# Offloaded exponentials on VectorE and GpSimd: a cubic without a quadratic term, fraction passes that either engine may run, GpSimd work in halves, and 73 packs in place of 65

## The chip, the cores and the metric

The kernel runs on one core of one Trainium2 chip. The metric is the device time of one execution in microseconds (us). Times below are medians of several executions. A ratio is computed as the mean time of one kernel's fast runs over that of the other's fast runs of the same rounds, so it is not quite the ratio of the medians. The study calls a run slow when it is over 1.5% longer than the fastest of its kernel.

A core has five engines that matter here. In this kernel TensorE multiplies matrices into PSUM. ScalarE evaluates the exponential. VectorE does elementwise work. GpSimd does elementwise work too, on SBUF tiles alone. SyncE issues DMAs. In the profile they are called PE, ACT, DVE, POOL and SP.

## The reference

Two attention branches share one input x (2048 x 512, 32 heads of 16) and are mixed by a gate. Branch A, softmax attention, is almost all of the work.

```
g = sigmoid((x * gate_w).sum(-1))
a = softmax_attention(x, A_wqkv, A_wo)      # 32 heads x 2048 x 2048 exponentials
b = linear_attention(x, B_wqkv, B_w_phi, B_wo)
out = g * a + (1 - g) * b
```

## The kernel before

Scores are computed in units of one head, 128 keys and 512 queries. For most units ScalarE takes the exponential straight from PSUM (`ps_ring` to `ET`), three units and two units in turn. That is 2048 units in all, too much for ScalarE alone to be fast: at the 0.452 us per unit that the profile below shows, an estimated 926 us. So four units at a time form a "pack" (128 x 2048) whose exponential is computed elsewhere, from the bits of the number. VectorE scales the scores into a 32-bit fixed-point number whose upper 16 bits are the exponent and whose lower 16 bits are the fraction (`EW`). GpSimd turns the upper half into bf16 bits (`ED`), VectorE extracts the fraction (`Ef`), evaluates a cubic in it (`Em`), and adds it to `ED`:

```python
ws.append(s.op("dve", 0.605, ... tensor_scalar(EW[i], bank, EC, 127*65536, mult, add)))   # x4, from PSUM
h  = s.op("pool", 1.9, ... tensor_scalar(ED, upper(EW), 128.0, EM, mult, add), ws, ...)   # integer part
f  = s.op("dve", 1.13, ... tensor_scalar(Ef, lower(EW), 2**-16, -EPHI, mult, add), ...)   # fraction
t  = s.op("dve", 0.6,  ... tensor_scalar(Em, Ef, E3, E2, mult, add))
u  = s.op("dve", 1.13, ... tensor_tensor(Em, Ef, Em, mult))
q  = s.op("dve", 0.6,  ... tensor_scalar(Em, Em, E1, add))
g_ = s.op("dve", 1.13, ... tensor_tensor(Em, Ef, Em, mult))
vs = s.op("dve", 1.13, ... tensor_tensor(ED, ED, Em, add), [g_, h])
...                                         # then TensorE multiplies ED with V
DVE_COUNT = (1, 1, 1, 2, 2, 2, 2, 1, 3, ...)      # packs in each of the 32 steps (4 heads x 512 queries); sum 65
```

(Abbreviated.) All instructions are placed by a planner that is part of the kernel. It is given a duration for each operation (the 0.605, 1.9, ... above), simulates the engines, and fixes the order of instructions on each engine when the kernel is built. The lists LEAD, PACE and BOUNDS say when work is released to it. In its plan a VectorE operation marked `port=True` and a GpSimd pass never run at the same time, and it holds GpSimd passes back until VectorE is about to do work that reads PSUM.

Two PSUM banks (`ps_mp`) serve everything but the main chain: the scores of packs, the projections, and the output matmuls.

The softmax here doesn't subtract the row's maximum and nothing guards it: scores larger than these inputs give would overflow.

## Time and profile before

| | before |
|---|---|
| time | 871.35 us (three runs, 870.81 to 872.87) |
| ScalarE busy | 842.7 us, 97% |
| VectorE busy | 796.9 us, 91% |
| GpSimd busy | 131.5 us, 15% |

The first part of the profile's page, the busy time of each engine with its share of the span, and the chain of work that ended last, by engine, for the kernel before:

```profile
PE 748.0 (86%) x5242; PEld 215.5 (25%) x5330; DVE 796.9 (91%) x1118; ACT 842.7 (97%) x783; POOL 131.5 (15%) x76
...
ACT 93%; PE 4%; DVE 1%; SPq 1%; DMA 1%; issue 0%; another core or an unknown queue 0%
```

The busy time alone would leave it open whether VectorE binds too. The chain does not: followed back from the last instruction, 93% of the span is ScalarE's own work. But the view by windows shows that VectorE has almost no room in the middle of the kernel (columns: window, its length, then the busy time of each engine, the clock, DMA share, GB/s):

```profile
core 0: us, PE busy (x) PEld busy (x) DVE busy (x) ACT busy (x) POOL busy (x), PEclk, DMA share, GB/s
...
200.00:300.00 100.00, 87.73 (x631) 25.36 (x640) 98.56 (x130) 100.00 (x103) 13.28 (x7) 1.00 0.01 3
...
600.00:700.00 100.00, 84.87 (x633) 25.23 (x642) 98.94 (x151) 100.00 (x93) 13.29 (x7) 1.00 0.02 6
```

Both engines are full there. What can be taken from ScalarE depends on what a pack costs VectorE. The groups of the page (line, engine, operation, tiles, shapes, count, then busy us, mean ns, and idle time before) give that cost:

```profile
L735 ACT ACTIVATE ET<-ps_ring 128x1536 bf16<-128x1536 f32 x715 | 817.5, 1346 | 10.8 <-PE ps_ring L718 9.2
...
L819 POOL TENSOR_SCALAR ED<-EW 128x2048 int16<-128x2048 int16 x65 | 124.4, 1915 | 717.4 <-DVE Em L829 101.5
L812 DVE TENSOR_SCALAR EW<-ps_mp 128x512 int32<-128x512 f32 x260 | 170.8, 680 | 11.7 <-PE ps_mp L808 9.0
...
L822 DVE TENSOR_SCALAR Ef<-EW 128x2048 f16<-128x2048 uint16 x65 | 83.3, 1282 | 0.5
L830 DVE TENSOR_TENSOR ED<-ED,Em 128x2048 uint16<-128x2048 int16 x65 | 81.3, 1251 | 0.5 <-POOL ED L819 0.2
L829 DVE TENSOR_TENSOR Em<-Ef,Em 128x2048 f16<-128x2048 f16 x65 | 81.1, 1247 | 0.5
L827 DVE TENSOR_TENSOR Em<-Ef,Em 128x2048 f16<-128x2048 f16 x65 | 79.3, 1220 | 0.4
...
L825 DVE TENSOR_SCALAR Em<-Ef 128x2048 f16<-128x2048 f16 x65 | 49.2, 757 | 0.4
L828 DVE TENSOR_SCALAR Em<-Em 128x2048 f16<-128x2048 f16 x65 | 47.3, 728 | 0.4
```

The seven VectorE groups add up to 592 us, or 9.1 us per pack. A pack takes four units of 512 columns from ScalarE. In steady state three units and two units follow each other every 2.26 us, so a unit costs ScalarE 0.452 us and a pack spares it 1.81 us.

The mean of 1282 ns for `Ef` hides two kinds. Here are three instructions from the timeline of the kernel before (start us, duration us, engine, line, operation), first of GpSimd, then of VectorE:

```profile
414.90 1.90 POOL L819 TENSOR_SCALAR ED<-EW 128x2048 int16<-128x2048 int16 x1 [10.57 <-DVE ED L830]
```

```profile
415.93 1.94 DVE L822 TENSOR_SCALAR Ef<-EW 128x2048 f16<-128x2048 uint16 x1
...
425.75 1.18 DVE L822 TENSOR_SCALAR Ef<-EW 128x2048 f16<-128x2048 uint16 x1
```

The pass at 425.75 us ran alone. The one at 415.93 us met a GpSimd pass and took 0.76 us longer; it ended 1.07 us after GpSimd did. I call this blocking. To count it, I took, for each group of equal instructions, the time above the group's lower quartile wherever it exceeded 60 ns: 21.2 us on VectorE in the kernel before. The 21.2 us lie on 28 VectorE instructions, each of which met a GpSimd pass. The `EW` passes, which read PSUM, show none of it: 120 of the 260 ran at least partly under a GpSimd pass, and none took over 0.693 us (median 0.681 us).

### The profile page before, as it was taken

To read this page: it belongs to the slowest core of one execution; us is meant where nothing else is said; L and a number is where in the kernel's file an instruction comes from. 1 tells how busy PE (TensorE), PEld (TensorE's weight loads), DVE (VectorE), ACT (ScalarE), POOL (GpSimd) and SP (SyncE) were. 2 spreads that over 40 slices of the span, in tenths; PEclk is the share of its full clock that TensorE was granted. 3 is DMA by queue.
4 is the path that set the end of the run, shared out by engine and by line. 5 is a ranking of instruction groups with operands and counts; after the bars stand their busy time and mean duration, and the time that the engine had idled before them with its cause. 6 is when DMAs were issued, how large, how long until landed. Compare 5 with 4: busy or idle time off the path is not lost.

```text
span 871.1 us, 12869 instructions
## 1 busy us (share of the span) xinstructions
PE 748.0 (86%) x5242; PEld 215.5 (25%) x5330; DVE 796.9 (91%) x1118; ACT 842.7 (97%) x783; POOL 131.5 (15%) x76
## 2 busy tenths in 40 slices
PE   6999998898888888888888888888788897878885
PEld 2323322222222222222222222222222221212221
DVE  2765799999999999979999998999999999999986
ACT  3999999999999999999999999999999999999995
POOL 3000111100110010120102111112100111212020
PEclk8999999999999999999999999999999999999998
DMA  5231000000000000000000000000000000000000
GB/s 109 62 76 52 4 4 3 2 4 5 3 2 4 4 4 8 10 10 10 4 2 9 4 17 9 5 3 2 4 4 10 10 10 8 3 4 4 4 1 25
DMA packets 25115, 11.21 MB, mean 13 GB/s; under 512 B 18016, under 2 KB 25056, under 8 KB 25056
## 3 DMA queue, kind: packets, MB, share of 16 engines
q1 hardware_dynamic: 23472, 9.99, 4.3%
q8 instruction: 42, 0.69, 0.3%
q10 hardware_dynamic: 1584, 0.39, 0.2%
q14 instruction: 17, 0.14, 0.1%
HBM read 3.16 MB, written 2.10 MB: 6 GB/s over the span
## 4 chain that ended last, share of the span: by engine, by line
ACT 93%; PE 4%; DVE 1%; SPq 1%; DMA 1%; issue 0%; another core or an unknown queue 0%
ACT ET L735 90%; ACT phi L958 4%; PE ps_ring L718 2%; PE ps_mp L605 1%; SPq L545 1%; PE ps_ot L763 1%; DMA xT<-in_A_x_dram 0%; DVE kvbd L938 0%; DMA out_dram<-outt 0%; DVE outt L1070 0%; DVE fsum L962 0%; DVE EW L812 0%; PE ps_ot L836 0%; DVE T L847 0%; PE ps_mp L896 0%
## 5 line engine op out<-in xcount | busy, mean ns | idle before, releaser
L735 ACT ACTIVATE ET<-ps_ring 128x1536 bf16<-128x1536 f32 x715 | 817.5, 1346 | 10.8 <-PE ps_ring L718 9.2
L718 PE MATMUL ps_ring<-qT,kT 64*128 64x512 bf16 x1788 | 357.1, 387 | 95.9 <-ACT ET L735 88.9
L819 POOL TENSOR_SCALAR ED<-EW 128x2048 int16<-128x2048 int16 x65 | 124.4, 1915 | 717.4 <-DVE Em L829 101.5
L812 DVE TENSOR_SCALAR EW<-ps_mp 128x512 int32<-128x512 f32 x260 | 170.8, 680 | 11.7 <-PE ps_mp L808 9.0
L763 PE MATMUL ps_ot<-ET,Vaug 128*17 128x512 bf16 x1788 | 176.1, 386 | 1.0 <-ACT ET L735 0.5
L718 PEld LDWEIGHTS ps_ring<-qT,kT 64*128 64x128 bf16 x1788 | 73.7, 93 | 300.2 <-ACT ET L735 260.2
L808 PE MATMUL ps_mp<-qT,kT 128*128 128x512 bf16 x221 | 83.2, 388 | 4.4 <-DVE EW L812 1.0
L822 DVE TENSOR_SCALAR Ef<-EW 128x2048 f16<-128x2048 uint16 x65 | 83.3, 1282 | 0.5
L830 DVE TENSOR_TENSOR ED<-ED,Em 128x2048 uint16<-128x2048 int16 x65 | 81.3, 1251 | 0.5 <-POOL ED L819 0.2
L829 DVE TENSOR_TENSOR Em<-Ef,Em 128x2048 f16<-128x2048 f16 x65 | 81.1, 1247 | 0.5
L827 DVE TENSOR_TENSOR Em<-Ef,Em 128x2048 f16<-128x2048 f16 x65 | 79.3, 1220 | 0.4
L763 PEld LDWEIGHTS ps_ot<-ET,Vaug 128*17 128x17 bf16 x1788 | 43.0, 87 | 141.4 <-issue 129.5
L825 DVE TENSOR_SCALAR Em<-Ef 128x2048 f16<-128x2048 f16 x65 | 49.2, 757 | 0.4
L828 DVE TENSOR_SCALAR Em<-Em 128x2048 f16<-128x2048 f16 x65 | 47.3, 728 | 0.4
L808 PEld LDWEIGHTS ps_mp<-qT,kT 128*128 128x128 bf16 x260 | 24.0, 96 | 64.0 <-issue 31.6
L964 DVE TENSOR_TENSOR phi<-phi,frec 128x1024 bf16<-128x1024 bf16 x32 | 39.2, 1225 | 0.1
L962 DVE TENSOR_REDUCE fsum<-phi 128x64 f32<-128x1024 bf16 x32 | 38.5, 1203 | 0.3 <-ACT phi L958 0.3
L605 PE MATMUL ps_mp<-xT,WA 128*128 128x512 bf16 x110 | 35.5, 388 | 3.7 <-DMA xT<-in_A_x_dram 2.5
L958 ACT ACTIVATE phi<-ps_mp 128x512 bf16<-128x512 f32 x64 | 38.6, 723 | 0.0
L605 PE MATMUL ps_mp<-Wp,xT 128*128 128x512 bf16 x115 | 37.4, 384 | 1.2 <-DVE EW L812 0.5
L662 DVE CAST Vaug<-ps_mp 128x128 bf16<-128x128 f32 (+1 forms) x32 | 13.4, 423 | 17.3 <-PE ps_mp L605 17.1
L847 DVE STREAM_TRANSPOSE T<-ps_ot 128x512 f32<-128x512 f32 x32 | 22.7, 710 | 6.7 <-PE ps_ot L763 6.2
(70 smaller groups left out, 425.7 us busy)
## 6 DMA issues: line engine op xcount, KB each, us to landing
out_dram<-outt SPq DMA_DIRECT2D x16, 128.0 KB, 1.7
qT<-qst SPq DMA_DIRECT2D x120, 16.0 KB, 1.8
WA<-in_A_wqkv_dram SPq DMA_DIRECT2D x3, 384.0 KB, 4.6
WBV<-in_B_wqkv_dram SPq DMA_DIRECT2D x1, 512.0 KB, 4.1
WoA<-in_A_wo_dram SPq DMA_DIRECT2D x1, 512.0 KB, 3.6
WoB<-in_B_wo_dram SPq DMA_DIRECT2D x1, 512.0 KB, 4.3
WA<-in_A_wqkv_dram ACTq DMA_DIRECT2D x3, 128.0 KB, 3.3
xT<-in_A_x_dram SPq DMA_TRANSPOSE x16, 2.7
```

The source lines that it names most:

```text
L605: m = s.op("pe", self.c_mm(n), lambda e, c=c: e.matmul(self.bk(b)[:, 0:n], lhs(c), rhs(c), start=(c == 0), stop=(c == 3)), deps if c == 0 ...
L718: return lambda e: e.matmul(self.ps_ring[:, x % RING, :], self.kT[r, g // 2, kt * P:(kt + 1) * P], self.qT[r, n % 2, i, :], start=True, st ...
L735: self.o_exp.append(s.op("act", w * 0.434 + 0.045, lambda e, b0=b0, s0=s0, w=w: e.activation(self.ET[:, s0:s0 + w, :], self.ps_ring[:, b0: ...
L763: return lambda e: e.matmul(self.ps_ot[32 * i:32 * i + VSL, :], self.Vaug[:, kt, h, :], self.ET[:, (4 * p + k) % NSLOT, :], start=(kt == 0 ...
L808: m = s.op("pe", self.c_mm(512), lambda e, i=i, b=b: e.matmul(self.bk(b), self.kT[:, cp, kt * P:(kt + 1) * P], self.qT[:, n % 2, i, :], st ...
L812: ws.append(s.op("dve", 0.605, lambda e, i=i, b=b: e.tensor_scalar(self.EW[:, ew.idx, i * QCH:(i + 1) * QCH], self.bk(b), float(EC), float ...
L819: h = s.op("pool", 1.9, lambda e: e.tensor_scalar(out().bitcast(dt.int16), half(1, dt.int16), 128.0, float(EM), op0=ALU.mult, op1=ALU.add) ...
L822: f = s.op("dve", 1.13, lambda e: e.tensor_scalar(self.Ef[:], half(0, dt.uint16), float(2.0 ** -16), -EPHI, op0=ALU.mult, op1=ALU.add), ws ...
L827: u = s.op("dve", 1.13, lambda e: e.tensor_tensor(self.Em[:], self.Ef[:], self.Em[:], ALU.mult), [t], pr, port=True)
L829: g_ = s.op("dve", 1.13, lambda e: e.tensor_tensor(self.Em[:], self.Ef[:], self.Em[:], ALU.mult), [q], pr, port=True)
L830: vs = [s.op("dve", 1.13, lambda e: e.tensor_tensor(out(), out().bitcast(dt.int16), self.Em[:], ALU.add), [g_, h], pr, port=True)]
L958: ex.append(s.op("act", 0.478, lambda e, sg=sg: e.activation(self.phi[:, ph.idx, :, sg, :], self.bk(b).rearrange("p (h f) -> p h f", f=DH) ...
```

## The change

The intent is to make a pack cheap enough on VectorE that eight more packs can be taken from ScalarE. There are five parts.

1. The cubic is expanded about its inflection point, so that it has no quadratic term: u(E1 + E3 u²) with u = fraction + 0.965. One scale-add pass on VectorE goes away; the constant moves into EM.
2. The fraction pass may run on GpSimd or VectorE (`alt=0.6`), whichever the planner finds free; `Ef` gets a second buffer.
3. GpSimd passes are issued in halves of 1024 columns.
4. 73 packs instead of 65, with new plan constants and new rules (RULES) for holding and releasing GpSimd passes.
5. The first of the eight output matmuls of a tile (seven and one in the last four tiles) waits for the operands of the whole sum.

```diff
-LEAD = [16.9408, 8.9394, 19.7683, 21.1253, 20.1566]
-PACE = [7.9948, 0.4589]
-BOUNDS = [5.8136, 10.5124, 10.0461, 26.2873]
+LEAD = [16.392310765238605, 9.228976317877777, 20.2802, 21.11011600354882, 19.952522408464993]
+PACE = [7.244074408835803, 0.4535348430560933]
+BOUNDS = [5.884433981907029, 10.4896, 10.2757, 27.4904]
+RULES = [0.9369, 0.1308, 0.8252]
-EM = 53
-EPHI = 0.49984589
-E1, E2, E3 = 125.48413, 43.840203, 9.9574722
+EM = -68
+EU = 0.96498297
+E1, E3 = 61.15205816, 9.99312212
-DVE_COUNT = (1, 1, 1, 2, 2, 2, 2, 1, 3, 2, 1, 3, 1, 2, 3, 1, 2, 3, 2, 2, 2, 2, 3, 2, 1, 3, 2, 2, 4, 1, 3, 3)
+DVE_COUNT = (1, 1, 1, 2, 2, 3, 2, 2, 2, 1, 3, 3, 1, 3, 3, 2, 2, 3, 3, 2, 3, 2, 2, 2, 4, 2, 3, 2, 3, 2, 3, 3)
 ... (planner: an operation may have a second engine; rules for releasing GpSimd passes)
-        h = s.op("pool", 1.9, lambda e: e.tensor_scalar(
-            out().bitcast(dt.int16), half(1, dt.int16), 128.0, float(EM), op0=ALU.mult, op1=ALU.add), ws, pr, ...)
-        f = s.op("dve", 1.13, ... self.Ef[:], half(0, dt.uint16), float(2.0 ** -16), -EPHI, ...)
-        t = s.op("dve", 0.6, lambda e: e.tensor_scalar(
-            self.Em[:], self.Ef[:], E3, E2, op0=ALU.mult, op1=ALU.add), [f], pr, port=True)
-        u = s.op("dve", 1.13, ... tensor_tensor(self.Em[:], self.Ef[:], self.Em[:], ALU.mult), [t], ...)
-        q = s.op("dve", 0.6, ... tensor_scalar(self.Em[:], self.Em[:], E1, None, op0=ALU.add), [u], ...)
+        fs = [s.op("pool", 0.98, lambda e, c=c: e.tensor_scalar(
+            self.Ef[:, ef.idx, W * c:W * c + W], half(0, dt.uint16, c), float(2.0 ** -16), EU,
+            op0=ALU.mult, op1=ALU.add), ws[2 * c:2 * c + 2], pr, alloc=[ef], frees=[ew], gate=gate, alt=0.6,
+            port=True) for c in range(2)]
+        hs = [s.op("pool", 0.98, ... self.ED half c ... ws[2 * c:2 * c + 2], ...) for c in range(2)]
+        u = s.op("dve", 1.13, lambda e: e.tensor_tensor(self.Em[:], Ef(), Ef(), ALU.mult), fs + [self.ed_prev], ...)
+        q = s.op("dve", 0.6, lambda e: e.tensor_scalar(
+            self.Em[:], self.Em[:], E3, E1, op0=ALU.mult, op1=ALU.add), [u], pr, port=True)
 ... (outputs)
-                    ... alloc=[b, *also] if k == 0 else (), order=[m], cols=512,
+                    ... alloc=[b, *also] if k == 0 else (), order=[m] if k else [x[3] for x in bl],
```

More of the change, by code (lines that the diff above doesn't have):

```diff
@@ L28 @@
 PASSES = 1
-LEAD = [16.9408, 8.9394, 19.7683, 21.1253, 20.1566]
-PACE = [7.9948, 0.4589]
-BOUNDS = [5.8136, 10.5124, 10.0461, 26.2873]
+LEAD = [16.392310765238605, 9.228976317877777, 20.2802, 21.11011600354882, 19.952522408464993]
+PACE = [7.244074408835803, 0.4535348430560933]
+BOUNDS = [5.884433981907029, 10.4896, 10.2757, 27.4904]
+RULES = [0.9369, 0.1308, 0.8252]
 VSL = 17
 EC = 0.25 * 1.4426950408889634 * 65536
-EM = 53
-EPHI = 0.49984589
-E1, E2, E3 = 125.48413, 43.840203, 9.9574722
-DVE_COUNT = (1, 1, 1, 2, 2, 2, 2, 1, 3, 2, 1, 3, 1, 2, 3, 1, 2, 3, 2, 2, 2, 2, 3, 2, 1, 3, 2, 2, 4, 1, 3, 3)
+EM = -68
+EU = 0.96498297
+E1, E3 = 61.15205816, 9.99312212
+DVE_COUNT = (1, 1, 1, 2, 2, 3, 2, 2, 2, 1, 3, 3, 1, 3, 3, 2, 2, 3, 3, 2, 3, 2, 2, 2, 4, 2, 3, 2, 3, 2, 3, 3)
 def dve_tiles(n):
-    return ((6,), (5, 11), (4, 8, 12), (3, 6, 9, 12))[DVE_COUNT[min(n, NN - 1)] - 1]
+    return ((6,), (5, 11), (4, 8, 12), (3, 6, 9, 12), (2, 5, 8, 11, 13))[DVE_COUNT[min(n, NN - 1)] - 1]
 class Buf:
@@ L61, in __init__ @@
         self.left = readers
+        self.war = ()
         self.last = []
@@ L73 @@
                  "ready", "seq", "dma", "order", "inc", "tick", "clock", "war", "cols", "lat", "cfg", "exp", "grp", "port",
-                 "gate", "go")
+                 "gate", "go", "alt", "run")
     def __init__(self, eng, dur, fns, deps, prio, rel, alloc, frees, dma, order, cols=0, cfg="F", port=False,
-                 gate=False):
+                 gate=False, alt=0.0, run=0.0):
         self.cols = cols
+        self.alt = alt
+        self.run = run or dur
         self.port = port or eng == "pool"
@@ L109, in __init__ @@
     def __init__(self):
+        self.SHY, self.REST, self.FILL = RULES
         self.ops = []
@@ L117, in op @@
     def op(self, eng, dur, fns, deps=(), prio=0.0, rel=0.0, alloc=(), frees=(), dma=0, order=(),
-           cols=0, cfg="F", port=False, gate=False):
+           cols=0, cfg="F", port=False, gate=False, alt=0.0, run=0.0):
         if not isinstance(fns, (list, tuple)):
@@ L122, in op @@
             cols = 90
-        o = Op(eng, dur, list(fns), deps, prio, rel, alloc, frees, dma, order, cols, cfg, port, gate)
+        o = Op(eng, dur, list(fns), deps, prio, rel, alloc, frees, dma, order, cols, cfg, port, gate, alt, run)
         if eng == "dve" and any(getattr(b.pool, "scarce", False) for b in o.frees):
@@ L173, in run, with at, push, release @@
         self.exps = [q.exp for q in self.chain]
-        def release(o):
+        def at(o, eng):
             r = o.rel
             for d in list(o.deps) + list(o.order):
-                if d.eng == o.eng and not d.dma:
-                    r = max(r, d.end + (self.RAW[o.eng] if d in o.deps else 0.0))
+                if d.eng == eng and not d.dma:
+                    r = max(r, d.end + (self.RAW[eng] if d in o.deps else 0.0))
                 else:
                     r = max(r, self.seen(d))
-            o.ready = r
-            heapq.heappush(future[o.eng], (r, o.seq, o))
+            return r
+        def push(o, when=0.0):
+            heapq.heappush(future[o.eng], (max(when, at(o, o.eng)), o.seq, o))
+            if o.alt:
+                heapq.heappush(future["dve"], (max(when, at(o, "dve") + self.SHY), o.seq, o))
+        def release(o):
+            o.ready = at(o, o.eng)
+            push(o)
         for o in self.ops:
@@ L191, in run @@
             for e in self.ENGS:
+                while ready[e] and ready[e][0][2].start is not None:
+                    heapq.heappop(ready[e])
+                while future[e] and future[e][0][2].start is not None:
+                    heapq.heappop(future[e])
                 if ready[e]:
@@ L206, in run @@
             now, e = best
+            if parked and not ready["dve"] and now >= t["dve"] and now >= hold["pool"] and (
+                    not future["dve"] or future["dve"][0][0] - now > self.REST * parked[0].dur):
+                c = parked.pop(0)
+                c.go = True
+                if last is not None:
+                    c.war.append(last)
+                heapq.heappush(future["pool"], (now, c.seq, c))
+                continue
             if e == "pe":
@@ L224, in run @@
                 c = it[2]
+                if c.start is not None:
+                    continue
                 if look is not None and c is not look[0]:
@@ L233, in run @@
                 if e == "pool" and c.gate and not c.go:
-                    parked.append(c)
+                    if c not in parked:
+                        parked.append(c)
                     continue
-                if e == "dve" and c.port and hold["pool"] > now + 0.02 and len(held) < 8:
+                if e == "dve" and c.port and hold["pool"] > now + 0.02:
                     held.append(it)
@@ L242, in run @@
                 continue
-            if e == "dve" and o is None and held:
-                o = held[0][2]
-                held = held[1:]
+            if e == "dve" and o is None:
+                for it in held:
+                    heapq.heappush(future[e], (hold["pool"], it[1], it[2]))
+                continue
             if o is None:
@@ L263, in run @@
                 if pool.free[0][0] > now:
-                    heapq.heappush(future[e], (pool.free[0][0], o.seq, o))
+                    push(o, pool.free[0][0])
                     ok = False
@@ L268, in run @@
                 continue
+            if e != o.eng:
+                o.eng, o.dur = e, o.alt
+                if o in parked:
+                    parked.remove(o)
             for b in o.alloc:
-                _, b.idx, war = b.pool.free.pop(0)
-                o.war.extend(war)
+                if b.idx is None:
+                    _, b.idx, b.war = b.pool.free.pop(0)
+                o.war.extend(b.war)
             if o.port:
@@ L276, in run @@
             if e == "dve":
-                while o.gate and parked:
-                    c = parked.pop(0)
-                    c.go = True
-                    if last is not None:
-                        c.war.append(last)
-                    heapq.heappush(future["pool"], (now + self.TAIL["dve"], c.seq, c))
+                if parked and not o.port:
+                    free = o.run + sum(x[2].run for x in ready[e] if not x[2].port and x[2].start is None)
+                    free -= max(0.0, hold["pool"] - now)
+                    while parked and free > self.FILL * parked[0].dur:
+                        c = parked.pop(0)
+                        c.go = True
+                        if last is not None:
+                            c.war.append(last)
+                        heapq.heappush(future["pool"], (now + self.TAIL["dve"], c.seq, c))
+                        free -= c.dur
                 last = o
@@ L307, in run @@
                     for q in b.pool.parked:
-                        heapq.heappush(future[q.eng], (ft, q.seq, q))
+                        push(q, ft)
                     b.pool.parked = []
@@ L462, in memory @@
         at("EW", [P, 2, 4 * QCH], dt.int32)
-        at("Ef", [P, 4 * QCH], dt.float16)
+        at("Ef", [P, 2, 4 * QCH], dt.float16)
         at("Em", [P, 4 * QCH], dt.float16)
@@ L489, in pools @@
         self.ED_p = BufPool(2)
+        self.Ef_p = BufPool(2)
         self.outt_p = BufPool(3)
@@ L802, in dve_pack @@
         pr = rel + LEAD[1]
-        ew, ed = Buf(self.EW_p, 2), Buf(self.ED_p, 1)
+        ew, ed, ef = Buf(self.EW_p, 4), Buf(self.ED_p, 1), Buf(self.Ef_p, 2)
         ws = []
@@ L813, in dve_pack @@
                 self.EW[:, ew.idx, i * QCH:(i + 1) * QCH], self.bk(b), float(EC), float(127 * 65536),
-                op0=ALU.mult, op1=ALU.add), [m], pr, frees=[b], gate=i < 2))
+                op0=ALU.mult, op1=ALU.add), [m], pr, frees=[b], run=0.605 * (4 - i)))
             self.qk_dve[n] = self.eq_prev = m
-        half = lambda k, t: self.EW[:, ew.idx, :].bitcast(t).rearrange("p (n two) -> p n two", two=2)[:, :, k]
+        W = 2 * QCH
+        half = lambda k, t, c: self.EW[:, ew.idx, W * c:W * c + W].bitcast(t).rearrange(
+            "p (n two) -> p n two", two=2)[:, :, k]
@@ L817, in dve_pack @@
         out = lambda: self.ED[:, ed.idx, :]
-        h = s.op("pool", 1.9, lambda e: e.tensor_scalar(
-            out().bitcast(dt.int16), half(1, dt.int16), 128.0, float(EM), op0=ALU.mult, op1=ALU.add), ws, pr,
-            alloc=[ed], frees=[ew], gate=(n, j) != (NN - 1, nj - 1))
-        f = s.op("dve", 1.13, lambda e: e.tensor_scalar(
-            self.Ef[:], half(0, dt.uint16), float(2.0 ** -16), -EPHI, op0=ALU.mult, op1=ALU.add),
-            ws + [self.ed_prev], pr, frees=[ew], port=True)
@@ L825, in dve_pack @@
-        t = s.op("dve", 0.6, lambda e: e.tensor_scalar(
-            self.Em[:], self.Ef[:], E3, E2, op0=ALU.mult, op1=ALU.add), [f], pr, port=True)
-        u = s.op("dve", 1.13, lambda e: e.tensor_tensor(self.Em[:], self.Ef[:], self.Em[:], ALU.mult), [t], pr, port=True)
-        q = s.op("dve", 0.6, lambda e: e.tensor_scalar(self.Em[:], self.Em[:], E1, None, op0=ALU.add), [u], pr, port=True)
-        g_ = s.op("dve", 1.13, lambda e: e.tensor_tensor(self.Em[:], self.Ef[:], self.Em[:], ALU.mult), [q], pr, port=True)
@@ L830, in dve_pack @@
-        vs = [s.op("dve", 1.13, lambda e: e.tensor_tensor(out(), out().bitcast(dt.int16), self.Em[:], ALU.add), [g_, h], pr,
-                   port=True)]
+        Ef = lambda: self.Ef[:, ef.idx, :]
+        gate = (n, j) != (NN - 1, nj - 1)
+        fs = [s.op("pool", 0.98, lambda e, c=c: e.tensor_scalar(
+            self.Ef[:, ef.idx, W * c:W * c + W], half(0, dt.uint16, c), float(2.0 ** -16), EU,
+            op0=ALU.mult, op1=ALU.add), ws[2 * c:2 * c + 2], pr, alloc=[ef], frees=[ew], gate=gate, alt=0.6,
+            port=True) for c in range(2)]
@@ new lines, in dve_pack @@
+        hs = [s.op("pool", 0.98, lambda e, c=c: e.tensor_scalar(
+            self.ED[:, ed.idx, W * c:W * c + W].bitcast(dt.int16), half(1, dt.int16, c), 128.0, float(EM),
+            op0=ALU.mult, op1=ALU.add), ws[2 * c:2 * c + 2], pr, alloc=[ed], frees=[ew], gate=gate)
+            for c in range(2)]
+        u = s.op("dve", 1.13, lambda e: e.tensor_tensor(self.Em[:], Ef(), Ef(), ALU.mult), fs + [self.ed_prev], pr,
+                 frees=[ef], port=True)
+        q = s.op("dve", 0.6, lambda e: e.tensor_scalar(
+            self.Em[:], self.Em[:], E3, E1, op0=ALU.mult, op1=ALU.add), [u], pr, port=True)
@@ L832, in dve_pack @@
+        g_ = s.op("dve", 1.13, lambda e: e.tensor_tensor(self.Em[:], Ef(), self.Em[:], ALU.mult), [q], pr,
+                  frees=[ef], port=True)
+        vs = [s.op("dve", 1.13, lambda e: e.tensor_tensor(out(), out().bitcast(dt.int16), self.Em[:], ALU.add),
+                   [g_] + hs, pr, port=True)]
         self.ed_prev = vs[-1]
@@ L1038, in mms @@
                     self.bk(b), src(), W[:, pr, :], start=(k == 0), stop=(k == len(bl) - 1)),
-                    [dep, self.d_woa, self.d_wob], prio, rel, alloc=[b, *also] if k == 0 else (), order=[m], cols=512,
-                    frees=[ba] if ba else ())
+                    [dep, self.d_woa, self.d_wob], prio, rel, alloc=[b, *also] if k == 0 else (), order=[m] if k else [x[3] for x in bl],
+                    cols=512, frees=[ba] if ba else ())
             return m
```

## The prediction

> **What bounds the kernel now.** ScalarE, with VectorE nearly as full. The page's busy table gives ScalarE 842.7 us of 871.1 (97%), VectorE 796.9 (91%), TensorE 748.0, GpSimd 131.5 (15%). The chain that ended last is 93% ScalarE (90% the exponential ET from ps_ring). From 100 to 840 us the windows view shows ScalarE 97 to 100%, VectorE 91 to 99% busy. So exponentials can be moved off ScalarE only if each offloaded pack first becomes cheaper on VectorE. In the timeline, a group of three and a group of two exponentials repeat every 2.26 us: 0.452 us per 512 columns.
>
> **VectorE cost per pack (65 packs), by the groups view.** Old: EW 4 passes, 170.8/65 = 2.63 us; Ef 1.28; Em scale-add 0.76; product 1.22; add 0.73; product 1.25; final add 1.25. Sum 9.1 us, 593 us in all. The new cubic, expanded at its inflection point, has no quadratic term: one scale-add pass goes, and the fraction pass Ef may run on GpSimd. New per pack: 2.63 + 1.22 + 0.73 + 1.25 + 1.25 = 7.1 us, plus about 1.4 us (estimate: two halves) if VectorE extracts the fraction. For 73 packs: 517 us with all fractions on GpSimd, 619 us with none. VectorE total between 721 and 823 us against 797 now. Likely about 760.
>
> **GpSimd.** Half of the 1.90 us pass is an estimated 0.98 us. Integer parts 73 x 1.96 = 143 us; with half of the fractions about 215 us. GpSimd stays below 35% busy, but blocks VectorE. [...] an Ef pass starting at 415.93 us, under a GpSimd pass (414.90 to 416.80), took 1.94 us instead of 1.18; a T product at 847.66 took 2.10 instead of 0.42. Means above the undisturbed durations give some 20 us of such blocking now; I expect 15 to 40 us after. VectorE can absorb that.
>
> **On the critical path.** Eight more packs take 32 x 512 columns from ScalarE: 32 x 0.452 = 14.5 us. All of it is on the chain, since ScalarE is the bottleneck throughout. The idle parts of ScalarE should stay: some 15 us before the first exponential, about 6 us of waits, about 11 us of tail after the last exponential. The VectorE relief only pays for the packs. TensorE work hardly changes. The changed ordering of the output matmuls keeps a half-done accumulation from blocking TensorE, worth at most 1 us.
>
> **Predicted: 856.5 us** (871.35 - 14.5, rounded), range 851 to 864. Chances: faster by over 2% (below about 854 us) 0.25; within 2% 0.72; slower 0.03.
>
> **What would show the steps right.** about 703 exponential instructions instead of 715; ScalarE busy near 828 us, share still 97%; the period still 2.26 us; ScalarE waits in the chain unchanged at 5 to 8 us; GpSimd busy 180 to 260 us; VectorE busy 745 to 800 us; one Em pass gone; Ef split between the engines.
>
> **What would make it wrong.** Slower: [...] packs or PSUM banks come late, TensorE stops in order at them, and ScalarE waits more than 10 us on ps_ring. Or GpSimd halves cost far over 0.98 us. Faster: the new plan also removes start-up waits or the stall near 323 us, where kvbd took 2.0 us and ScalarE then waited 1.6 us.

(The sum came to 871.35 - 14.5 = 856.9, put down as 856.5 us. Two durations were estimates. For half of the 1.90 us GpSimd pass it took 0.98 us; the changed kernel's trace shows 1.04 us. For a fraction extracted by VectorE in two halves it took 1.4 us, with `Ef` whole at a mean of 1.28 us; there the trace shows 2 x 0.68 us.)

## The result, and the profile after

The changed kernel took 855.85 us (four runs, 854.87 to 856.81) against 871.08 us for the kernel before. The ratio is 0.9825, with a 95% interval of 0.9811 to 0.9840. That is faster by 1.75%, clear of noise, and inside the predicted range.

| | before | after |
|---|---|---|
| time | 871.08 us | 855.85 us |
| span of the profiled run | 871.1 us | 854.7 us |
| ScalarE busy | 842.7 us | 828.2 us |
| ScalarE not busy (span less busy) | 28.4 us | 26.5 us |
| VectorE busy | 796.9 us | 767.0 us |
| GpSimd busy | 131.5 us | 280.1 us |
| time lost to blocking, VectorE / GpSimd | 21.2 / 1.1 us | 21.5 / 24.7 us |

The busy time of each engine and the chain that ended last, in the changed kernel:

```profile
PE 744.6 (87%) x5226; PEld 215.1 (25%) x5316; DVE 767.0 (90%) x1105; ACT 828.2 (97%) x771; POOL 280.1 (33%) x250
...
ACT 92%; PE 4%; DVE 1%; SPq 1%; POOL 1%; DMA 1%; issue 0%; ACTq 0%
```

The groups that answer to those shown of before:

```profile
L774 ACT ACTIVATE ET<-ps_ring 128x1536 bf16<-128x1536 f32 (+1 forms) x703 | 803.0, 1345 | 8.6 <-PE ps_ring L757 8.0
...
L865 POOL TENSOR_SCALAR ED<-EW 128x1024 int16<-128x1024 int16 x146 | 173.8, 1199 | 322.6 <-DVE Em L873 64.1
L851 DVE TENSOR_SCALAR EW<-ps_mp 128x512 int32<-128x512 f32 x292 | 192.4, 680 | 25.3 <-PE ps_mp L847 18.3
L861 POOL TENSOR_SCALAR Ef<-EW 128x1024 f16<-128x1024 uint16 x93 | 99.3, 1067 | 235.0 <-DVE EW L851 58.0
...
L869 DVE TENSOR_TENSOR Em<-Ef 128x2048 f16<-128x2048 f16 x73 | 93.6, 1282 | 2.8 <-POOL Ef L861 2.5
L875 DVE TENSOR_TENSOR ED<-ED,Em 128x2048 uint16<-128x2048 int16 x73 | 92.4, 1266 | 2.5 <-POOL ED L865 2.3
L873 DVE TENSOR_TENSOR Em<-Ef,Em 128x2048 f16<-128x2048 f16 x73 | 92.8, 1271 | 0.6
...
L871 DVE TENSOR_SCALAR Em<-Em 128x2048 f16<-128x2048 f16 x73 | 55.7, 763 | 0.2
...
L861 DVE TENSOR_SCALAR Ef<-EW 128x1024 f16<-128x1024 uint16 x53 | 36.0, 680 | 0.0
```

Read the first line against that of before: 703 exponentials instead of 715, and 803.0 us instead of 817.5. The difference is 14.5 us, which is the saving forecast for 32 units. The mean duration of one is the same (1345 and 1346 ns), so ScalarE was not slowed by its neighbours. One `Em` group is gone. Of 146 fraction halves, GpSimd ran 93 and VectorE 53. The five VectorE groups and the VectorE share of `Ef` add up to 563 us, 7.7 us per pack. VectorE does eight packs more and is 30 us less busy.

GpSimd's half pass takes 1.04 us when it is alone, but the integer passes average 1199 ns, and the longest took 2.08 us. This is why (timeline of the changed kernel; GpSimd, then VectorE):

```profile
781.71 3.02 POOL L865 TENSOR_SCALAR ED<-EW 128x1024 int16<-128x1024 int16 x2
```

```profile
782.46 1.37 DVE L875 TENSOR_TENSOR ED<-ED,Em 128x2048 uint16<-128x2048 int16 x1
```

The first line merges two GpSimd passes; the second of them started at 782.72 us and took 2.01 us, under a VectorE add with two SBUF inputs that had started 0.26 us earlier. In the kernel before, GpSimd hardly ever lost time so (1.1 us in all); in the changed one it loses 24.7 us. What VectorE loses to GpSimd did not grow (21.5 us, on 51 instructions, each of which met a GpSimd pass). The `EW` passes again show none of it: 204 of the 292 ran at least partly under a GpSimd pass, and none took over 0.694 us. GpSimd's loss was not quite free. These are later lines of that timeline, for TensorE's score matmul of a pack, which needs the `EW` buffer that the delayed pass was reading, and for ScalarE:

```profile
784.79 0.39 PE L847 MATMUL ps_mp<-qT,kT 128*128 128x512 bf16 x1 [1.30 <-POOL ED L865]
...
785.75 1.45 ACT L774 ACTIVATE ET<-ps_ring 128x1536 bf16<-128x1536 f32 x1 [0.77 <-PE ps_ring L757]
```

TensorE stood for 1.30 us and ScalarE then for 0.77 us. This is part of the 1% that the chain of the changed kernel puts down to POOL.

### The profile page after: what moved, and what is told of

The parts are those of the page before. It is cut to its first block, busy times and chain, and to the rows that moved or that the text cites. A ratio compares the mean times of both kernels' runs of the same rounds, so it can differ in the third digit from the quotient of the medians.

```text
span 854.7 us, 13035 instructions
## 1 busy us (share of the span) xinstructions
PE 744.6 (87%) x5226; PEld 215.1 (25%) x5316; DVE 767.0 (90%) x1105; ACT 828.2 (97%) x771; POOL 280.1 (33%) x250
## 4 chain that ended last, share of the span: by engine, by line
ACT 92%; PE 4%; DVE 1%; SPq 1%; POOL 1%; DMA 1%; issue 0%; ACTq 0%
ACT ET L774 88%; ACT phi L1003 4%; PE ps_ring L757 2%; PE ps_mp L644 1%; SPq L584 1%; PE ps_ot L802 1%; POOL ED L865 0%; DMA xT<-in_A_x_dram 0%; PE ps_mp L847 0%; POOL Ef L861 0%; DVE EW L851 0%; DMA out_dram<-outt 0%; DVE outt L1115 0%; PE ps_mp L1082 0%; DVE Em L869 0%
## 5 line engine op out<-in xcount | busy, mean ns | idle before, releaser
L774 ACT ACTIVATE ET<-ps_ring 128x1536 bf16<-128x1536 f32 (+1 forms) x703 | 803.0, 1345 | 8.6 <-PE ps_ring L757 8.0
L865 POOL TENSOR_SCALAR ED<-EW 128x1024 int16<-128x1024 int16 x146 | 173.8, 1199 | 322.6 <-DVE Em L873 64.1
L851 DVE TENSOR_SCALAR EW<-ps_mp 128x512 int32<-128x512 f32 x292 | 192.4, 680 | 25.3 <-PE ps_mp L847 18.3
L861 POOL TENSOR_SCALAR Ef<-EW 128x1024 f16<-128x1024 uint16 x93 | 99.3, 1067 | 235.0 <-DVE EW L851 58.0
L847 PE MATMUL ps_mp<-qT,kT 128*128 128x512 bf16 x245 | 92.2, 390 | 6.8 <-DVE EW L851 1.7
L869 DVE TENSOR_TENSOR Em<-Ef 128x2048 f16<-128x2048 f16 x73 | 93.6, 1282 | 2.8 <-POOL Ef L861 2.5
L875 DVE TENSOR_TENSOR ED<-ED,Em 128x2048 uint16<-128x2048 int16 x73 | 92.4, 1266 | 2.5 <-POOL ED L865 2.3
L873 DVE TENSOR_TENSOR Em<-Ef,Em 128x2048 f16<-128x2048 f16 x73 | 92.8, 1271 | 0.6
L861 DVE TENSOR_SCALAR Ef<-EW 128x1024 f16<-128x1024 uint16 x53 | 36.0, 680 | 0.0
L881 PE MATMUL ps_ot<-ED,Vaug 128*17 128x512 bf16 x292 | 29.1, 392 | 1.2 <-DVE ED L875 1.1
```

The source lines that it names most:

```text
L774: self.o_exp.append(s.op("act", w * 0.434 + 0.045, lambda e, b0=b0, s0=s0, w=w: e.activation(self.ET[:, s0:s0 + w, :], self.ps_ring[:, b0: ...
L847: m = s.op("pe", self.c_mm(512), lambda e, i=i, b=b: e.matmul(self.bk(b), self.kT[:, cp, kt * P:(kt + 1) * P], self.qT[:, n % 2, i, :], st ...
L851: ws.append(s.op("dve", 0.605, lambda e, i=i, b=b: e.tensor_scalar(self.EW[:, ew.idx, i * QCH:(i + 1) * QCH], self.bk(b), float(EC), float ...
L861: fs = [s.op("pool", 0.98, lambda e, c=c: e.tensor_scalar(self.Ef[:, ef.idx, W * c:W * c + W], half(0, dt.uint16, c), float(2.0 ** -16), E ...
L865: hs = [s.op("pool", 0.98, lambda e, c=c: e.tensor_scalar(self.ED[:, ed.idx, W * c:W * c + W].bitcast(dt.int16), half(1, dt.int16, c), 128 ...
L869: u = s.op("dve", 1.13, lambda e: e.tensor_tensor(self.Em[:], Ef(), Ef(), ALU.mult), fs + [self.ed_prev], pr, frees=[ef], port=True)
```

## The experiments

Twelve kernels were run, and all twelve gave correct outputs. Where it is said that plan constants were "searched anew", the kernel's planner was run by itself with about a thousand random changes of LEAD, PACE, BOUNDS, RULES and the pack counts (their sum fixed), and the constants with the earliest planned end were taken. That is a shorter search than the changed kernel's own constants may have had, so a time of such a kernel is an upper bound for its idea. The two kernels measured first ended 7.6 and 7.8 us later than the planner planned; the expectations use this.

The theory was: ScalarE's exponentials set the time, and everything done to VectorE and GpSimd only makes room for more packs. One rival was that VectorE, at 98% in the middle, binds as well, so that lighter packs shorten the time by themselves. The other was that the replanning gave the gain.

| run | what differs | median us | ratio to before (95%) |
|---|---|---|---|
| changed kernel | | 855.85 | 0.9825 (0.9811 to 0.9840) |
| e1 | 65 packs | 872.14 | 1.0004 (0.9967 to 1.0040) |
| e2 | old arithmetic, 73 packs | 900.96 | 1.0337 (1.0309 to 1.0366) |
| e3 | quadratic term back | 868.59 | 0.9972 (0.9943 to 1.0002) |
| e4 | fractions on VectorE only | 867.69 | 0.9949 (0.9889 to 1.0009) |
| e5 | fractions on GpSimd only | 855.51 | 0.9827 (0.9801 to 0.9853) |
| e6 | passes not halved | 862.65 | 0.9918 (0.9880 to 0.9956) |
| e7 | 81 packs | 874.00 | 1.0036 (1.0009 to 1.0064) |
| e8 | plan constants of before | 866.28 | 0.9938 (0.9913 to 0.9962) |
| e9 | 75 packs | 853.48 | 0.9790 (0.9768 to 0.9813) |
| e10 | planner with measured durations | 852.87 | 0.9782 (0.9767 to 0.9797) |
| e11 | changed kernel again | 854.66 | 0.9797 (0.9782 to 0.9813) |
| e12 | output order undone | 867.27 | 0.9953 (0.9940 to 0.9967) |

Differences of a few us need one more look. The mean clock that TensorE was granted (as a share of full speed) differs between executions of one kernel, and the time goes with it: the five runs of e11 took 852.83 and 852.97 us at 0.996, 855.12 at 0.992, 854.66 at 0.991 and 856.81 at 0.987. What sets the clock, and whether a kernel's own stalls lower it, no run here shows. Where it matters, runs at like clock are compared below.

Each part of the change was undone on its own, except the new rules for GpSimd passes (RULES and the planner's code for them) and the second `Ef` buffer.

### e1: everything but the extra packs

```diff
-DVE_COUNT = (1, 1, 1, 2, 2, 3, 2, 2, 2, 1, 3, 3, 1, 3, 3, 2, 2, 3, 3, 2, 3, 2, 2, 2, 4, 2, 3, 2, 3, 2, 3, 3)
+DVE_COUNT = (1, 1, 1, 2, 2, 2, 2, 1, 3, 2, 1, 3, 1, 2, 3, 1, 2, 3, 2, 2, 2, 2, 3, 2, 1, 3, 2, 2, 4, 1, 3, 3)
```

> The changed kernel with the pack counts of before (65 packs instead of 73), nothing else. Theory ScalarE: the time follows the exponentials that ScalarE keeps, so 32 x 512 columns return and the time is 855.9 + 14.5 = 870.4 us (869 to 872), with VectorE about 60 us less busy than in the changed kernel (near 705 us) and no benefit from it. Rival VectorE: lighter packs shorten a VectorE-bound program by themselves; the time stays near 856 to 862. Rival plan: the new plan parameters and the new order of the output matmuls gave the gain; the time stays near 856 to 860.

It took 872.14 us, the time of the kernel before. The busy time of each engine in e1:

```profile
PE 752.1 (86%) x5294; PEld 218.4 (25%) x5382; DVE 721.3 (83%) x1046; ACT 843.2 (97%) x783; POOL 232.5 (27%) x213
```

VectorE is 76 us less busy than in the kernel before, at the same number of packs, and this bought nothing: ScalarE is at 843.2 us again, and the time with it. Both rivals fall in the form stated. VectorE's fullness was not a second bound on the time; it was the bound on how many packs could be moved. And the planner changes alone are worth nothing at 65 packs. The constants were those for 73 packs and not searched anew, but this cannot hide much: ScalarE's time not busy was 28.4 us (span 871.6 us), just as in the kernel before.

### e2: the extra packs without the new arithmetic

The kernel before, with

```diff
-DVE_COUNT = (1, 1, 1, 2, 2, 2, 2, 1, 3, 2, ...)    # sum 65
+DVE_COUNT = (...)                                   # sum 73, searched anew with LEAD, PACE, BOUNDS
-                    ... order=[m], cols=512,
+                    ... order=[m] if k else [x[3] for x in bl], cols=512,
```

(One step has five packs, for which a fifth list of positions was added.)

> The kernel before, with its old polynomial and whole GpSimd passes, but 73 packs, the new output-matmul order (without it the planner does not find a schedule) and plan constants searched anew for this case. Theory ScalarE with VectorE as the limit on the pack count: VectorE would need 797 + 8 x 9.1 = 870 us of work, so the packs come late and the time is above 880 us; the kernel's own planner, plus the 7.7 us by which both measured kernels exceed it, gives about 904. If the new arithmetic were not needed and only the pack count mattered: about 857 us.

It took 900.96 us. The busy time of each engine, ScalarE's waits (who waited for whom: us in total, times, longest), the starts of three ScalarE instructions in the timeline, with the idle time before them, and TensorE's lines just before the second of them:

```profile
PE 763.3 (85%) x5366; PEld 221.7 (25%) x5458; DVE 861.2 (96%) x1198; ACT 829.5 (92%) x771; POOL 146.1 (16%) x84
```

```profile
ACT ET L735 <- PE ps_ot L763: 34.3, 11, 11.0
```

```profile
358.92 15.93 ACT L735 ACTIVATE ET<-ps_ring 128x1024 bf16<-128x1024 f32 x14 [7.75 <-PE ps_ot L763]
...
732.07 27.49 ACT L735 ACTIVATE ET<-ps_ring 128x1536 bf16<-128x1536 f32 x24 [10.96 <-PE ps_ot L763]
864.40 1.45 ACT L735 ACTIVATE ET<-ps_ring 128x1536 bf16<-128x1536 f32 x1 [9.66 <-PE ps_ot L763]
```

```profile
731.41 0.10 PEld L836 LDWEIGHTS ps_ot<-ED,Vaug 128*17 128x17 bf16 x4 [0.42 <-DVE ED L830]
...
731.63 0.39 PE L763 MATMUL ps_ot<-ET,Vaug 128*17 128x512 bf16 x4
```

ScalarE has its 829.5 us, as in the changed kernel, but it stands still for long stretches. In the planned order the last products with V of a step (`ps_ot`) come after those of its packs. At 731.41 us TensorE took up a pack that VectorE had just finished (`ED`), at 731.63 us the product from `ET` behind it, and with that ScalarE, idle for 10.96 us, could go on at 732.07 us: while a pack is late, the `ET` tiles that ScalarE writes are not freed. VectorE is at 861 us, 96% of the span. So packs are only worth having if VectorE finishes them in time.

### e3: the quadratic term back

```diff
-        u = s.op("dve", 1.13, ... tensor_tensor(self.Em[:], Ef(), Ef(), ALU.mult), fs + [self.ed_prev], ...)
-        q = s.op("dve", 0.6, ... tensor_scalar(self.Em[:], self.Em[:], E3, E1, op0=ALU.mult, op1=ALU.add), ...)
+        t = s.op("dve", 0.6, ... tensor_scalar(self.Em[:], Ef(), E3, E2, op0=ALU.mult, op1=ALU.add), fs + [self.ed_prev], ...)
+        u = s.op("dve", 1.13, ... tensor_tensor(self.Em[:], Ef(), self.Em[:], ALU.mult), [t], ...)
+        q = s.op("dve", 0.6, ... tensor_scalar(self.Em[:], self.Em[:], E1, None, op0=ALU.add), [u], ...)
```

(with the old EM, E1, E2, E3 and fraction offset, and constants searched anew)

> The changed kernel with the old polynomial (quadratic term back: one more 0.68 us VectorE pass in each of 73 packs, +50 us), plan constants searched anew. Theory: the saved pass is what pays for the packs; VectorE would need about 817 us of 856 and cannot place it all in time; planner plus 7.7 us gives about 870. If VectorE had enough slack (767 of 855 us busy in the changed kernel): about 857.

It took 868.59 us: nearly the whole gain is lost with one 0.7 us pass per pack (the lower quartile of such a scale-add in the kernel before is 0.68 us). VectorE was busy 814.3 us, 94% of the span, and ScalarE's waits for `ps_ot` were 7.2 us.

### e4 and e5: who extracts the fraction

```diff
 e4:
-        fs = [s.op("pool", 0.98, ... alloc=[ef], frees=[ew], gate=gate, alt=0.6, port=True) for c in range(2)]
+        fs = [s.op("dve", 0.6, ... alloc=[ef], frees=[ew], port=True) for c in range(2)]
 e5:
-        ... alloc=[ef], frees=[ew], gate=gate, alt=0.6,
+        ... alloc=[ef], frees=[ew], gate=gate,
```

> The changed kernel with every fraction pass on VectorE (GpSimd only the integer parts, in halves), plan constants searched anew. Theory: 93 halves x 0.6 us = 56 us come back to VectorE[...]; VectorE needs about 815 us; planner plus 7.7 us gives about 866. If the freedom to use GpSimd for fractions is not needed: 856 to 858.

> The changed kernel with every fraction pass on GpSimd (the planner may not move one to VectorE), nothing else. Theory: VectorE still has room and GpSimd works 306 us of 855, so the choice of engine is worth nothing more at 73 packs: 856 to 858 us (planner plus 7.7 us: 856.8). [...]

(Cut from the first text is a term for time that VectorE would get back from GpSimd, given by a mechanism that no run shows; the sum is 767 + 56 = 823 us, and with the cut term "about 815". Its 0.6 us for a half is the planner's duration; the changed kernel's trace shows 0.68 us. Cut from the second text is a rival that rested on the same mechanism. What it forecast can be tested without it: 53 more half passes on GpSimd, 55 us at 1.04 us each, delay VectorE, and the time rises above 862 us.)

With all fractions on VectorE (e4) the time was 867.69 us, VectorE busy 804.0 us. With all of them on GpSimd (e5) it was 855.51 us, the same as the changed kernel. (The clock was low in some runs of e4. At like clock its loss is nearer 10 us: 867.20 us at 0.988, against 856.81 us at 0.987 in e11.) So GpSimd must take fractions, but at 73 packs the free choice between the engines is worth nothing measurable. e5 also answers that rival: GpSimd was busy 347.6 us, and the blocking rose to 29.7 us on VectorE and 35.9 us on GpSimd (same count as above), yet the time stayed, because VectorE as a whole was at 747.4 us and had room.

### e6: GpSimd passes not halved

```diff
-        W = 2 * QCH
+        W = 4 * QCH
-        fs = [s.op("pool", 0.98, ... ws[2 * c:2 * c + 2], ... alt=0.6, port=True) for c in range(2)]
+        fs = [s.op("pool", 1.9, ... ws, ... alt=1.13, port=True) for c in range(1)]
```

(the integer passes likewise; constants searched anew)

> The changed kernel with GpSimd passes (and the fraction passes on VectorE) over all 2048 columns instead of halves, plan constants searched anew. Theory: a 1.9 us pass seldom fits between VectorE instructions [...], and a pack waits for all four EW passes first; planner plus 7.7 us gives about 863. If halving does not matter: 856 to 858. If fewer GpSimd instructions (less fixed cost) help: below 855.

(Cut is a clause on which VectorE instructions leave no room for a GpSimd pass; no run shows it.)

It took 862.65 us, 6.8 us more than the changed kernel. Halving matters, though a longer search might close part of this. The blocking was smaller here (15.7 us on VectorE, 7.3 us on GpSimd, in its slowest run, with 227.1 us of GpSimd work), so the halves do not help by avoiding blocking. That they help because they fit smaller gaps and can start after two of the four `EW` passes was not tested apart.

### e7 and e9: more packs

Only the pack counts and the constants searched for them differ from the changed kernel.

```diff
-DVE_COUNT = (...)   # sum 73
+DVE_COUNT = (...)   # e7: sum 81; e9: sum 75
```

> The changed kernel with 81 packs (8 more), plan constants searched anew. ScalarE loses another 14.5 us. If the time followed ScalarE alone: 841.4. Theory: 73 packs are near the point where both engines are full; VectorE would need 767 + 8 x 7.8 = 829 us, packs come late, and the planner plus 7.7 us gives about 873.

> The changed kernel with 75 packs, plan constants and counts searched anew. Theory: ScalarE loses 2 x 1.81 = 3.6 us more and VectorE can just hold it (767 + 2 x 7.8 = 783 us): between 852 and 855 us, planner plus 7.7 us gives 853.4. If the true limit is already reached at 73: 856 or more.

With 81 packs the time was 874.00 us. ScalarE's own work fell to 816.7 us, but its waits for `ps_ot`, which were 0.6 us in the changed kernel, came to

```profile
ACT ET L774 <- PE ps_ot L802: 21.4, 13, 4.9
```

in ScalarE's waits of e7: late packs, as in e2. With 75 packs (e9) it was 853.48 us, against 854.66 us for the changed kernel (e11). The intervals of the two ratios overlap, so a gain is not shown by the medians. At like clock e9 was the faster one: 850.45 us at 0.996 (e11 852.83 and 852.97) and 852.92 us at 0.992 (e11 855.12). A straight line through time and clock, with one slope for the 13 runs of e9, e10 and e11, puts e9 1.9 us below e11 (standard error 0.3 us). So 75 packs are probably better than 73, by less than the 3.6 us that ScalarE is spared; the best count lies below 81.

### e8 and e12: the plan and the order of the output matmuls

```diff
 e8:
-LEAD, PACE, BOUNDS = (of the changed kernel)
+LEAD, PACE, BOUNDS = (of the kernel before; RULES stay)
 e12:
-                    ... order=[m] if k else [x[3] for x in bl],
+                    ... order=[m], cols=512,
```

> The changed kernel with the plan constants of before (LEAD, PACE, BOUNDS), work per engine unchanged. Theory: ScalarE has the same 828 us of work, but the constants time the releases for 65 packs, so instructions come in a worse order and ScalarE waits several us more; planner plus 7.7 us gives 863. If the constants do not matter: 856.

> The changed kernel with only the new order of the output matmuls undone (the first of eight may start before the last operand is there), constants not searched anew. If, as the prediction said, the order is worth at most 1 us: 855 to 857. If the half-filled accumulation holds one of the two scratch banks long enough to disturb the plan: planner plus 7.7 us gives 869.

e8 took 866.28 us: with the same instructions, the constants are worth 10.4 us by the medians. Three of its four runs had a clock of 0.984, lower than any of the changed kernel. Its run at 0.990 took 863.12 us, that of the changed kernel at 0.990 856.49 us, so some 7 us stand at like clock; whether the old constants also bring the lower clock about is not known. The two parts of the change belong together: 73 packs need a plan made for 73 packs.

e12 took 867.27 us, 12.6 us more than e11. Here the traces show exactly where. Up to 632 us, every twentieth exponential of e12 starts within 0.1 us of the same one in the changed kernel. Then come these lines of TensorE's timeline in e12, all of its output matmuls from 769.6 us to 800 us:

```profile
769.61 0.38 PE L1082 MATMUL ps_mp<-WoA,onT_A 128*128 128x512 bf16 x1
770.46 0.39 PE L1082 MATMUL ps_mp<-WoA,onT_A 128*128 128x512 bf16 x1
799.63 1.04 PE L1082 MATMUL ps_mp<-WoA,onT_A 128*128 128x512 bf16 x2
```

From 763.7 to 770.8 us TensorE issued all but the last matmul of two sums (six of seven each; the eighth follows later). The last ones need `onT_A` of a step that is not yet finished; they run at 799.63 us. Between 770.9 and 799.6 us the timeline has no matmul into `ps_mp` at all: both banks hold half-finished sums, and no pack can begin. The windows view of e12, then of the changed kernel, shows what VectorE does in the meantime:

```profile
771.00:799.60 28.60, 21.67 (x168) 4.96 (x166) 12.76 (x18) 28.39 (x26) 2.06 (x2) 0.95 0.02 4
```

```profile
771.00:799.60 28.60, 22.07 (x149) 5.19 (x151) 23.87 (x31) 26.96 (x25) 12.26 (x10) 0.94 0.02 4
```

VectorE works 12.76 us in e12 and 23.87 us in the changed kernel, so 11 us of pack work is put off. ScalarE is not yet touched (28.39 us busy). The bill comes 35 us later, in ScalarE's timeline of e12:

```profile
834.31 1.45 ACT L774 ACTIVATE ET<-ps_ring 128x1536 bf16<-128x1536 f32 x1 [9.31 <-PE ps_ot L802]
```

The kernel before had long-held banks too (one tile from 801.5 us, a second from 812.8 us, the first of them ended only at about 823 us), but not for 29 us with both, and without a ScalarE wait. So the new order, which looks like a detail, takes a hazard out of the plan. Whether constants searched for e12 would avoid the stall stays open.

### e10 and e11: does a better-informed planner beat the changed kernel?

```diff
-            self.d_x.append(dma("sp", [... 4 transposing loads ...], QCH * D * 2, 0.84))
+            self.d_x.append(dma("sp", [... 4 transposing loads ...], 1, 1.3))
-        fs = [s.op("pool", 0.98, ...)      # hs likewise
+        fs = [s.op("pool", 1.1, ...)
-        bd = s.op("dve", 0.6, ...)         # kvbd
+        bd = s.op("dve", 1.92, ...)
```

(constants searched anew)

> The changed kernel, 73 packs, with four durations of its planner set to what the traces show (transposing load of x 1.3 us each instead of 0.84; GpSimd half 1.1 us instead of 0.98; kvbd 1.92 us instead of 0.6) and plan constants searched anew. Theory: ScalarE's work is unchanged, so at most the waits of ScalarE (8.6 us in the changed kernel) shrink: 853 to 856 us.

> The changed kernel itself again, as the yardstick for the other three on the same chip: 855 to 857 us.

(Of the durations given to the planner: in the changed kernel's trace the 16 transposing loads of x follow each other within 20.77 us, 1.30 us each, and two GpSimd half passes back to back start 1.12 us apart, at 452.50 and 453.62 us.)

ScalarE's waits in e11, then in e10:

```profile
ACT ET L774 <- PE ps_ring L757: 8.8, 5, 4.3
...
ACT ET L774 <- PE ps_ot L802: 0.6, 2, 0.4
```

```profile
ACT ET L774 <- PE ps_ring L757: 3.8, 4, 2.1
...
ACT ET L774 <- PE ps_ot L802: 0.4, 1, 0.4
```

In the profiled runs the waits shrank from 9.4 us to 4.2 us, at equal ScalarE work (828.0 and 828.3 us). Not all of that is the plan: e11's profiled run was the slowest of its five. The clock stood at 0.50 from 14 to 20 us and from 786 to 791 us, and 4.5 us of its waits end in these stretches or just after them; e10 had one such stretch (596 to 601 us), with 1.7 us. Of the rest, the first wait is the largest part: 4.3 us in e11, 2.1 us in e10. The medians differ by 1.8 us (854.66 and 852.87), and the intervals of the ratios just overlap. The straight line named under e9 puts e10, too, 1.9 us below e11 (standard error 0.3 us). e10 beats the kernel before by 2.2%; that it beats the changed kernel by about 2 us is likely, but was not tested in runs made for it. One of the durations given to the planner was also wrong, as the next section tells.

## Why the prediction was right

**The sum.** The prediction was 871.35 - 14.5 = 856.9, rounded to 856.5 us; measured 855.85. Its one large term, 32 units x 0.452 us on ScalarE, is confirmed twice: by ScalarE's busy time (842.7 to 828.2 us) and by e1, which gives the term back (872.14 us). The further 1.9 us between the profiled spans is ScalarE's idle time, 28.4 against 26.5 us; that is within the scatter of a kernel's own runs.

**VectorE only pays for the packs.** This held. e1 shows it from one side (76 us of relief, no gain), e2, e3 and e4 from the other (without the relief, most of what the packs spare is lost, and in e2 more than all of it). Predicted VectorE busy time 745 to 800 us, measured 767.0. Predicted blocking 15 to 40 us on VectorE, measured 21.5.

**GpSimd was mis-sized.** Predicted 180 to 260 us busy, about 215; measured 280.1. The terms: a half pass takes 1.04 us, not 0.98; GpSimd took 93 of 146 fraction halves, not half of them; and what GpSimd itself loses under VectorE's instructions, 24.7 us, was left out. That a half pass costs more than half of a whole one can be read from both traces: 1.897 us for 2048 columns and 1.044 us for 1024 leave, by estimate, 0.19 us that does not shrink with the columns. 239 passes x 1.044 us = 250 us, plus 24.7 us, plus 7.0 us of fills at the start, make 281 us. The prediction asked what GpSimd does to VectorE, but not what VectorE does to GpSimd. It cost little: at least one blocked pass reached ScalarE (0.77 us at 785.75 us), and e5 shows that even 348 us of GpSimd work leaves the time as it is.

**The order of the output matmuls was mis-sized.** The prediction called it "worth at most 1 us", a guess for which it gave no figure of the trace. Within this plan it is worth 12.6 us (e12): without it both scratch banks are held for 29 us, and ScalarE later stands still for 9.31 us.

**The plan constants were not considered.** The prediction took it for granted that idle time stays as it is when packs are added. e8 shows that this is bought: with the old constants the same instructions take 10.4 us longer (some 7 us at like clock). The prediction was right about the time because the constants had been searched well, and it had no grounds for that. Its chance of a slower result (3%) had no better grounds: e3 and e4 lost most of the gain and e7 all of it, and e2 was slower by 3.4%.

**One reading of the profile was half wrong.** The prediction named the `kvbd` product, which "took 2.0 us", as a stall that a new plan might remove. It is not a slow instruction. In the timeline of the kernel before (VectorE, then GpSimd) it lies under a GpSimd pass:

```profile
320.89 2.00 DVE L938 TENSOR_TENSOR kvbd<-kvacc,m 128x512 bf16<-128x512 f32 x1
```

```profile
320.45 1.90 POOL L819 TENSOR_SCALAR ED<-EW 128x2048 int16<-128x2048 int16 x1 [10.65 <-DVE kvacc L934]
```

and among the groups of the changed kernel, where it runs from 319.13 to 319.80 us with no GpSimd pass between 317.67 and 320.33 us, it takes 677 ns:

```profile
L983 DVE TENSOR_TENSOR kvbd<-kvacc,m 128x512 bf16<-128x512 f32 x1 | 0.7, 677 | 0.0
```

Its 2.00 us were mostly blocking: GpSimd's pass ended at 322.35 us, the product 0.54 us later. That ScalarE waited because of it was read rightly: the next `EW` pass could start only at 322.91 us, TensorE had stood 1.57 us for it at 323.65 us, and ScalarE 1.58 us at 324.89 us. So the 1.92 us given to the planner in e10 were a blocked duration and not the cost of the instruction. Before a single long instruction is called slow, look at what GpSimd was doing meanwhile: here the difference was 2.00 us against 0.68 us.

## What to carry to other kernels

When two engines are both full, find out which one the chain of work runs through. Here the other set only how much could be moved off the first, and the passes saved there were worth nothing until the saved room was spent (e1: 76 us less on VectorE, 872.14 us, the time of before). The price of one more piece moved rose steeply here once the second engine was full: the step from 65 to 73 pieces gave 15 us, and eight more lost 18. Differences of a few us between two such plans should be read at like granted clock (e11: 852.83 us at 0.996, 856.81 at 0.987). In a kernel with a fixed order of instructions, make the order anew for each such step (e8, with the old constants: 10.4 us by the medians, some 7 at like clock), and let no accumulation begin in a scarce PSUM bank before all its operands are there (e12: both banks held for 29 us, 12.6 us longer).
